# Another order of the seven products of a quad, with folds, scores and combines put at other places, in a channel-attention and squared-ReLU kernel

## The chip, the cores and the metric

The kernel runs on one core of one Trainium2 chip. The metric is device time in microseconds (us) of one execution; of several executions the median counts. One further execution was taken by the hardware profiler, and everything said of engines comes from that one.

## What is computed

For each of four batches a channel attention over 256 channels is followed by a two-layer network with a squared ReLU. Cut to what matters:

```python
qn = q / (norm(q, axis=1) + 1e-6)          # q, k, v: 4 x 6080 x 256
kn = k / (norm(k, axis=1) + 1e-6)
s = kn.transpose(0, 2, 1) @ qn / tau       # 256 x 256 for a batch: the "scores"
a = softmax(s)
x = (v @ a).reshape(24320, 256)
r = maximum(x @ w_in, 0.0)                 # w_in: 256 x 2048
return (r * r) @ w_out                     # w_out: 2048 x 256
```

## The kernel before

**Folding.** The softmax matrix of a batch has only 256 x 256 values, so the kernel never makes x. It multiplies the matrix into w_in (a *fold*) and then works with v and the folded weights. A fold handles one of four groups g of the weights and one of two halves; each half is six matmuls 512 columns wide (line 293).

**Quads and seven products.** The first layer is a 2 x 2 block product computed with seven products in place of eight (a Strassen-like scheme). `combine` (299) makes the seven weight combinations from a folded group, `v_combos` (343) those of v. A *quad* is one (chunk, j): a chunk is two runs of 512 tokens (480 in the last of a batch's six chunks), j counts eight pairs of 128-row blocks of the hidden layer. There are 4 x 6 x 8 = 192 quads. In a quad the functions `m1` to `m7` each issue one product of three matmuls, since every factor is split into a rounded high part and a remainder ("high by high, high by low, low by high"). They accumulate in the PSUM banks B (tile `h`), X (`x`) and Z (`z`), and m7 in a second `h` bank H. Tile pool `h` has two banks; folds, scores, norms and the transposes of the softmax take theirs from the same pool.

**From a product to the second layer.** `block` (381) takes bank X or Z through ReLU and square on ScalarE, then a rounding cast and a subtraction on VectorE, for the hidden blocks "11" and "12". For "21" and "22", `plus_m7` (430) adds m7 to banks B and Z on VectorE into the tile `s`, and `blocks` (392) makes high and low parts: VectorE 398, ScalarE 399, VectorE 400. I call this last sequence the **s chain**. `layer2` (453) multiplies a finished block of the *previous* quad by w_out: three matmuls for each of two halves e. So a quad has 7 x 3 + 8 x 3 = 45 matmuls, all issued in the order of the hand-written list `plan` (608): after each entry `run_side` (597) issues whatever side work is due, by a table of times in units of quads that is filled with `at(...)` (541 to 595).

**Side work.** For a batch that is to come, the scores (`score_burst`, line 182) need the key and query tiles loaded, squares of them summed for the norms (`score_norm`: ScalarE 152, VectorE 153), for batches 2 and 3 a high/low split (`score_split`: ScalarE 158, GpSimd 159), and matmuls (172); then norms, softmax, transposes, folds and combines. For batches 1 to 3 the combine, and the subtraction of `fold_split`, run on GpSimd; for batch 0 on VectorE. The four folds of a batch stand two quads apart, in quads 41, 43, 45 and 47 of the 48 of the batch before, both halves at 0.93 of a quad, followed at once by the combine. The weights w_in and w_out come as 64-bit floats and are decoded (lines 83 to 98) during the first seven quads.

**The head.** Before the first quad the 48 key tiles of batch 0 are scored in 12 groups of four, 1 MB each. Among them stand the decode of the first weight group and, on GpSimd, the combinations and splits of the first chunk of v. Three groups (`EARLY`) of batch 1 are also scored there, between the steps of the softmax; the other nine follow in quads 0 to 8. Loads are issued by SyncE's queue from the list `ring` (474), one after each group, into three buffers `kqt` and two `g2`.

The tile scheduler then reorders instructions within an engine, so their order there can differ from that of the code. On an engine a waiting instruction holds everything behind it.

Of the kernel before, what the change touches and what calls it, by code (L numbers as in the profile page):

```python
# [18 lines left out]
def tile_channel_attention_relu2_ffn(ctx, tc, kq, vT, tau, w_in, w_out, outT):  # L19
# [29 lines left out]
    EARLY = 3  # L49
# [32 lines left out]

    def decode_f64(raw, W):

        top = 122879.9921875
        shape = list(raw.shape[:3])
# [3 lines left out]
        nc.vector.tensor_scalar(out=hw, in0=raw[:, :, :, 1].bitcast(F32), scalar1=top, scalar2=-top,  # L90
                                op0=ALU.min, op1=ALU.max)
        nc.scalar.activation(out=mag, in_=hw, func=AF.Abs, scale=2.0 ** -112)
        nc.scalar.activation(out=low, in_=raw[:, :, :, 0], func=AF.Copy, scale=2.0 ** -29)
# [10 lines left out]
    def raw_tile():  # L104
        return work.tile([P, 2 * NH, GW, 2], U32, name="kqt", tag="kqt", bufs=KB)

    def load_w_in(g):
        raw = raws["in", g] = raw_tile()
        for h in range(NH):
            nc.sync.dma_start(out=raw[:, 2 * h:2 * h + 2].rearrange("p t n two -> p t (n two)"),  # L110
                              in_=wiv[:, h, :, 2 * g * GW:2 * (g + 1) * GW])
# [7 lines left out]
    def load_w_out(g):  # L119
        raw = raws["out", g] = raw_tile()  # L120
        for t in range(2):
            nc.sync.dma_start(out=raw[:, 2 * t:2 * t + 2].rearrange("p j n two -> p j (n two)"), in_=wov[:, g, t])

    def decode_w_out(g):
# [3 lines left out]
        nc.gpsimd.tensor_sub(out=wol[:, g], in0=W, in1=woh[:, g])  # L128
# [143 lines left out]
    def fold_split(b, g):  # L272
        W = win.pop((b, g))
        wi[b, g] = []
        for d in range(NH):
# [65 lines left out]
    ORDER = (A11, S2, A12, S3, A22, S1, S4)  # L341

    def v_combos(ci):

        T = chunks[ci][2]
        eng = nc.vector if ci else nc.gpsimd
# [10 lines left out]
        for i, x in ((A11, lambda: b11), (S2, lambda: t2), (A12, lambda: b21), (S3, lambda: diff(b22, b12)),  # L357
                     (A22, lambda: diff(b21, t2)), (S1, lambda: t1), (S4, lambda: b22)):
            yield ci, i, x

    def v_split(ci, i, x):
# [4 lines left out]
        (nc.vector if ci else nc.gpsimd).tensor_sub(out=t[:, 1, :T], in0=x, in1=t[:, 0, :T])  # L366
# [14 lines left out]
    def block(q, c, ps):  # L381
# [93 lines left out]
    for g in range(NGK):  # L475
        ring.append((score_load, 0, g, "g2" if g % 5 > 2 else "kqt"))
# [172 lines left out]
```

## Time and profile before

| | |
|---|---|
| three runs | 2275.04, 2277.61, 2281.0 us; median 2277.61 |
| the profiled execution | 2273.69 us, span 2271.7 us |
| mean granted TensorE clock | 0.994 |
| busy share of the span | TensorE 97%, VectorE 71%, ScalarE 57%, GpSimd 14% |
| moved by DMA | 329.36 MB, mean 145 GB/s |

The span runs from the first to the last instruction of the program; the 2 us beside it lie around it. "PE" is TensorE's matmul, "DVE" VectorE, "ACT" ScalarE, "POOL" GpSimd, "SP" SyncE, whose queue issues the DMAs. The busy share of PE counts overlapping pipelined matmuls, so time lost between them is partly hidden in the 97%; the prediction goes by counts of matmuls and their pace. In a row of the windows view stand the stretch, its length, then for each engine the busy time and in brackets the number of instructions, at the end the granted clock, the share of DMA engines in use and GB/s. In a row of the groups view stand line, engine, operation, tiles, shapes and count, then after the first bar the busy time of the group in us and the mean of one instruction in ns, and after the second bar the idle time of the engine ahead of them with what ended it.

### The profile page before, as it was taken

The page shows a single profiled execution, that of the slowest core. Times are in us where ns is not written, and L with a number is a line of the kernel's source. Part 1 is how long each engine was busy: PE and PEld are TensorE (multiplying, and loading weights), DVE is VectorE, ACT ScalarE, POOL GpSimd, SP SyncE. Part 2 cuts the span into 40 slices and gives each one's busy share as a digit, 9 for nine tenths or more (in the row PEclk, how much of TensorE's full clock was granted, in tenths as well). Part 3 has the DMA queues.
Part 4 walks back from the last instruction along what each step waited for, and adds up shares of the span by engine and source line. Part 5 has one row for each costly group of instructions (what it writes and reads, how often), then busy time and mean ns, then how long its engine had stood idle before and what let it go on. Part 6 is the DMA issues. An engine that isn't in the chain of part 4 may idle for free.

```text
span 2271.7 us, 25960 instructions
## 1 busy us (share of the span) xinstructions
PE 2199.5 (97%) x9848; PEld 1797.6 (79%) x9848; DVE 1621.8 (71%) x2160; ACT 1294.0 (57%) x2141; POOL 312.9 (14%) x262
## 2 busy tenths in 40 slices
PE   8799999999989999999998999999999999999999
PEld 7578777888868788888886878878887778888887
DVE  6777977567677877877758778787676676666665
ACT  5565755456565665655656556565465555555554
POOL 3000000000442111111053112121114100000000
PEclk9899999999999999999999999999999999999999
DMA  7656633233453433422346344243234432332321
GB/s 287 224 197 259 243 118 126 90 133 127 168 219 118 155 136 110 153 102 103 128 183 221 114 142 156 100 156 113 96 123 180 170 119 98 119 135 83 132 101 65
DMA packets 68860, 329.36 MB, mean 145 GB/s; under 512 B 7424, under 2 KB 11520, under 8 KB 61184
## 3 DMA queue, kind: packets, MB, share of 16 engines
q1 hardware_dynamic: 68736, 327.71, 40.3%
q8 instruction: 77, 1.26, 0.2%
q14 instruction: 47, 0.39, 0.1%
HBM read 271.32 MB, written 56.36 MB: 144 GB/s over the span
## 4 chain that ended last, share of the span: by engine, by line
PE 72%; DVE 8%; DMA 6%; ACT 6%; issue 4%; POOL 3%; SPq 0%; POOLq 0%; ACTq 0%; DVEq 0%
PE o L466 35%; PE h L378 17%; PE z L378 9%; PE x L378 5%; PE h L172 3%; DMA v<-vT 2%; DMA kqt<-kq 2%; DVE g L400 2%; PE h L293 2%; ACT g L399 1%; DMA wsc<-wt 1%; DVE vt L366 1%; POOL wt L315 1%; ACT r L387 1%; ACT r L386 1%
## 5 line engine op out<-in xcount | busy, mean ns | idle before, releaser
L466 PE MATMUL o<-g,woh 128*128 128x512 f32 (+1 forms) x3072 | 1077.1, 391 | 28.9 <-DVE g L400 19.4
L466 PEld LDWEIGHTS o<-g,woh 128*128 128x128 f32 x3072 | 576.8, 188 | 174.2 <-DVE g L400 36.2
L378 PE MATMUL h<-vt,wt 128*128 128x512 f32 (+1 forms) x2304 | 662.1, 391 | 7.7 <-ACT z L417 6.0
L466 PE MATMUL o<-g,wol 128*128 128x512 f32 (+1 forms) x1536 | 596.4, 388 | 1.7 <-POOL wol L128 1.7
L378 PEld LDWEIGHTS h<-vt,wt 128*128 128x128 f32 x2304 | 425.9, 188 | 100.1 <-ACT x L410 9.0
L388 DVE CAST g<-r 128x512 fp32r<-128x512 f32 (+1 forms) x384 | 187.3, 488 | 329.6 <-ACT r L387 328.0
L399 ACT CAST g<-s 128x1024 fp32r<-128x1024 f32 (+1 forms) x192 | 199.6, 1040 | 384.8 <-DVE s L398 384.5
L400 DVE TENSOR_TENSOR g<-s,g 128x1024 fp32r<-128x1024 f32 (+1 forms) x192 | 240.9, 1255 | 145.2 <-ACT g L399 144.9
L378 PE MATMUL z<-vt,wt 128*128 128x512 f32 (+1 forms) x1152 | 329.5, 394 | 12.3 <-DVE s L432 12.1
L466 PEld LDWEIGHTS o<-g,wol 128*128 128x128 f32 x1536 | 288.8, 188 | 58.6 <-POOL wol L128 2.1
L389 DVE TENSOR_TENSOR g<-r,g 128x512 fp32r<-128x512 f32 (+1 forms) x384 | 314.1, 818 | 10.2
L378 PEld LDWEIGHTS z<-vt,wt 128*128 128x128 f32 x1152 | 212.5, 188 | 69.4 <-DVE s L432 29.3
L387 ACT ACTIVATE r<-r 128x512 f32<-128x512 f32 (+1 forms) x384 | 240.5, 626 | 6.6
L398 DVE SCALAR_TENSOR_TENSOR s<-s 128x1024 f32<-128x1024 f32 (+1 forms) x192 | 236.1, 1230 | 5.0
L159 POOL TENSOR_TENSOR hl<-kqt,hl 128x512 fp32r<-128x512 f32 x96 | 139.2, 1463 | 655.8 <-ACT hl L158 655.8
L417 ACT COPY z<-h 128x512 f32<-128x512 f32 (+1 forms) x192 | 109.3, 569 | 192.8 <-PE h L378 191.9
L386 ACT ACTIVATE r<-z 128x512 f32<-128x512 f32 (+1 forms) x192 | 113.1, 589 | 118.7 <-PE z L378 118.7
L432 DVE TENSOR_TENSOR s<-h,m 128x512 f32<-128x512 f32 (+1 forms) x192 | 131.1, 683 | 53.2 <-PE h L378 52.4
L378 PE MATMUL x<-vt,wt 128*128 128x512 f32 (+1 forms) x576 | 164.5, 389 | 0.7 <-ACT x L410 0.7
L153 DVE TENSOR_TENSOR acc<-acc,sq 128x1024 f32<-128x1024 f32 x92 | 116.3, 1264 | 35.0 <-ACT sq L152 33.3
L432 DVE TENSOR_TENSOR s<-z,m 128x512 f32<-128x512 f32 (+1 forms) x192 | 130.7, 681 | 0.0
L386 ACT ACTIVATE r<-x 128x512 f32<-128x512 f32 (+1 forms) x192 | 113.6, 591 | 22.2 <-PE x L378 8.7
(107 smaller groups left out, 1689.6 us busy)
## 6 DMA issues: line engine op xcount, KB each, us to landing
wt<-wsc SPq DMA_DIRECT2D x184, 896.0 KB, 4.6
kqt<-kq SPq DMA_DIRECT2D x55, 1024.0 KB, 5.5
wsc<-wt SPq DMA_DIRECT2D x32, 896.0 KB, 4.5
v<-vT SPq DMA_DIRECT2D x40, 512.0 KB, 4.5
outT<-res SPq DMA_DIRECT2D x80, 256.0 KB, 2.6
kqt<-wins SPq DMA_DIRECT2D x12, 512.0 KB, 5.5
g<-kq SPq DMA_DIRECT2D x4, 1024.0 KB, 11.1
kqt<-w_in SPq DMA_DIRECT2D x8, 512.0 KB, 7.6
```

The source lines that it names most:

```text
L153: nc.vector.tensor_add(out=accs[b], in0=accs[b], in1=sq)
L159: nc.gpsimd.tensor_sub(out=hl[:, 1], in0=x, in1=hl[:, 0])
L378: nc.tensor.matmul(out=out[:, :T], lhsT=w[:, l, i], rhs=v[:, r, :T], start=start and n == 0, stop=n == 2, skip_group_check=True)
L386: nc.scalar.activation(out=r[:, :T], in_=ps[:, :T], func=AF.Relu)
L387: nc.scalar.activation(out=r[:, :T], in_=r[:, :T], func=AF.Square)
L388: nc.vector.tensor_copy(out=hl[:, 0, :T], in_=r[:, :T])
L389: nc.vector.tensor_sub(out=hl[:, 1, :T], in0=r[:, :T], in1=hl[:, 0, :T])
L398: nc.vector.scalar_tensor_tensor(out=s, in0=s, scalar=0.0, op0=ALU.max, in1=s, op1=ALU.mult)
L399: nc.scalar.copy(out=h, in_=s)
L400: nc.vector.tensor_sub(out=l, in0=s, in1=h)
L432: nc.vector.tensor_add(out=state[q]["s"][:, i, :T], in0=ps[:, :T], in1=state[q]["m7"][:, :T])
L466: nc.tensor.matmul(out=o[:, :T], lhsT=l[:, wg, wj, es], rhs=r[:, :T], start=first and k == 0, stop=last and k == 2)
```

## The change

- `plan` has another order. Before: m1, 11, 11, 21, m6, m2, 21, m7, 22, m4, m5, 22, 12, 12, m3. Now: m1, m7, 11, 11, m6, m2, 21, 21, m5, m4, 22, 22, 12, m3, 12 (the blocks are those of the previous quad, one entry for each half e). `blocks` is called from m4, now the later of the two. The v splits are put in the matching order.
- Folds and score bursts are issued at 0.46 of a quad in place of 0.93; the two halves of a fold of batches 1 to 3 stand in two neighbouring quads, and groups are four quads apart in place of two: quads 30 to 44 of a batch in place of 41 to 48. The scores of batches 2 and 3 and the norms of batch 1 end 9 to 11 quads earlier, so they stand closer: one pair of tiles in every quad from 2 to 25, in place of 24 pairs over 35 quads; batch 1's 24 norm steps lie in quads 10 to 25.
- Everything that GpSimd did, but for the score splits of batches 2 and 3, goes to VectorE: combines, `fold_split`'s subtraction, the low part of w_out, the first chunk's v combinations.
- The rounding cast of block "12" goes from VectorE to ScalarE.
- `EARLY` is 8: 32 key tiles of batch 1 are scored in the head. Only two of them stand ahead of the softmax steps, and the first chunk's v combinations are made behind the first combine. `w_in` and `w_out` of group 0 are loaded into buffers of v's pool in place of `kqt`, and `ring` has w_in at place 5 and v at 8.

The diff, cut to what the text speaks of:

```diff
-    EARLY = 3
+    EARLY = 8
...
+        if key[1]:
+            raw = work.tile([P, 2 * NH, GW, 2], U32, name="kqt", tag="kqt", bufs=KB)
...
+        else:
+            parts = raws[key] = [work.tile([P, 2, GW, 2], U32, name="vt", tag="vt", bufs=VB) for _ in range(2)]
...
-        nc.gpsimd.tensor_sub(out=wol[:, g], in0=W, in1=woh[:, g])
+        nc.vector.tensor_sub(out=wol[:, g], in0=W, in1=woh[:, g])
...
-            (nc.gpsimd if b else nc.vector).tensor_sub(out=w[:, 1], in0=x, in1=w[:, 0])
+            nc.vector.tensor_sub(out=w[:, 1], in0=x, in1=w[:, 0])
...
-        eng = nc.gpsimd if b else nc.vector
+        eng = nc.vector
         u = us.pop((b, g))
...
-        nc.vector.tensor_copy(out=hl[:, 0, :T], in_=r[:, :T])
+        eng(out=hl[:, 0, :T], in_=r[:, :T])
...
     def m4(q):
         product(q, A22, state[q]["B"], False)
-        state[q]["s"] = work.tile([P, 2, HMAX], F32, name="s", tag="s", bufs=1)
         plus_m7(q, 0, state[q]["B"])
+        blocks(q)
...
-        block(q, "12", state[q]["Z"])
+        block(q, "12", state[q]["Z"], nc.scalar.copy)
...
-        if g == NGK - 4:
-            for step in v_combos(0):
-                v_split(*step)
...
+    for step in v_combos(0):
+        v_split(*step)
     load_v(1)
-    early_mm(early[8:])
+    early_mm(len(early))
...
-    END = 0.93
+    MID = 0.46
...
-            at(u + END, score_burst, 1, list(range(i * G, i * G + G)))
+            at(u + MID + 0.001, score_burst, 1, list(range(i * G, i * G + G)))
...
-        first, last = (NJ + 3 if b == 1 else 2), QB - 11
+        first, last = (NJ + 2 if b == 1 else 2), 26
...
-            u = end + 2 + 2 * g
-            at(u - 0.9, load_win, b, g)
-            at(u + 0.4, fold_split, b, g)
-            at(u + END, fold, b, g, 0)
-            at(u + END, fold, b, g, 1)
-            at(u + 1.0, combine, b, g)
+            u = end + 4 + 4 * g
+            at(u - 1.5, load_win, b, g)
+            at(u - 0.5, fold_split, b, g)
+            at(u + MID, fold, b, g, 0)
+            at(u + 1 + MID, fold, b, g, 1)
+            at(u + 1.7, combine, b, g)
...
-    plan = (m1, ("11", 0), ("11", 1), ("21", 0), m6, m2, ("21", 1), m7, ("22", 0), m4, m5, ("22", 1), ("12", 0),
-            ("12", 1), m3)
+    plan = (m1, m7, ("11", 0), ("11", 1), m6, m2, ("21", 0), ("21", 1), m5, m4, ("22", 0), ("22", 1), ("12", 0),
+            m3, ("12", 1))
```

What the program has in a row afterwards is shown at three places. The names: `o` are the second layer's accumulators, `g` the high and low parts of a hidden block, `woh` and `wol` those of w_out, `hl` a split, `aTh` and `aTl` the transposed softmax, `u` (in a `kqt` or `vt` buffer) the folded weights, `sq` the combine's sums, `wt` the finished weights of a quad.

First, TensorE at the end of the head, from the last matmuls of the first fold (line 293, in the change 301) to the first products (378, in the change 384). The scores of batch 1 are the rows with `kqt` or `g` alone as their source. Before:

```order
L293 MATMUL h<-hl,aTl 128x512
L172 MATMUL o_374<-kqt 128x256 x8
L378 MATMUL h<-vt,wt 128x512 x3
L378 MATMUL x<-vt,wt 128x512 x3
L378 MATMUL h<-vt,wt 128x512 x9
```

And in the change:

```order
L301 MATMUL h<-hl,aTl 128x512
L179 MATMUL o_353<-kqt 128x256 x10
L179 MATMUL o_353<-g_310 128x256 x8
L179 MATMUL o_353<-g_351 128x256 x8
L384 MATMUL h<-vt,wt 128x512 x9
L384 MATMUL x<-vt,wt 128x512 x3
L384 MATMUL z<-vt,wt 128x512 x3
L384 MATMUL h<-vt,wt 128x512
L179 MATMUL o_353<-kqt 128x256 x8
```

Between the fold and the first product stand 26 score matmuls where 8 stood; another 8, and 16 more a little later, lie among the first quad's matmuls.

Second, TensorE in a quad without side work in the last batch, from m1 on. Before: m1, block 11 in both halves, the first half of block 21, m6, m2:

```order
L378 MATMUL h<-vt,wt 128x512 x3
L466 MATMUL o_16260<-g_16433,woh 128x512
L466 MATMUL o_16260<-g_16433,wol 128x512
L466 MATMUL o_16260<-g_16433,woh 128x512
L466 MATMUL o_16264<-g_16433,woh 128x512
L466 MATMUL o_16264<-g_16433,wol 128x512
L466 MATMUL o_16264<-g_16433,woh 128x512
L466 MATMUL o_16260<-g_16461,woh 128x512
L466 MATMUL o_16260<-g_16461,wol 128x512
L466 MATMUL o_16260<-g_16461,woh 128x512
L378 MATMUL h<-vt,wt 128x512 x3
L378 MATMUL x<-vt,wt 128x512 x3
```

And in the change (m1 and m7 in one row, block 11, m6, m2, the first half of block 21):

```order
L384 MATMUL h<-vt,wt 128x512 x6
L472 MATMUL o_16262<-g_16358,woh 128x512
L472 MATMUL o_16262<-g_16358,wol 128x512
L472 MATMUL o_16262<-g_16358,woh 128x512
L472 MATMUL o_16266<-g_16358,woh 128x512
L472 MATMUL o_16266<-g_16358,wol 128x512
L472 MATMUL o_16266<-g_16358,woh 128x512
L384 MATMUL h<-vt,wt 128x512 x3
L384 MATMUL x<-vt,wt 128x512 x3
L472 MATMUL o_16262<-g_16380,woh 128x512
L472 MATMUL o_16262<-g_16380,wol 128x512
L472 MATMUL o_16262<-g_16380,woh 128x512
```

The first rows of block 21 (source `g_16461` before, `g_16380` now), which need the s chain of the previous quad, stood as the fourth entry of the quad (behind nine matmuls) and stand as the seventh (behind eighteen).

Third, the second combine for batch 1. Before, GpSimd had it, one instruction behind the other:

```order
L307 TENSOR_TENSOR sq<-kqt 128x256
L305 TENSOR_TENSOR sq<-kqt 128x256
L306 TENSOR_TENSOR sq<-sq,kqt 128x256
L308 TENSOR_TENSOR sq<-kqt,sq 128x256
L315 TENSOR_TENSOR wt<-kqt,wt 128x256
L315 TENSOR_TENSOR wt<-kqt,wt 128x128
L315 TENSOR_TENSOR wt<-sq,wt 128x512
```

Now the same work stands on VectorE, among the s chain of a quad (lines 438, 404 and 406 in the change, 432, 398 and 400 before):

```order
L313 TENSOR_TENSOR sq<-kqt 128x256
L438 TENSOR_TENSOR s<-z,m_3778 128x512
L438 TENSOR_TENSOR s<-h,m_3778 128x512
L314 TENSOR_TENSOR sq<-sq,kqt 128x256
L404 SCALAR_TENSOR_TENSOR s<-s 128x1024
L316 TENSOR_TENSOR sq<-kqt,sq 128x256
L406 TENSOR_TENSOR g_3825<-s,g_3825 128x1024
L323 TENSOR_TENSOR wt<-kqt,wt 128x256
L323 TENSOR_TENSOR wt<-kqt,wt 128x128
L323 TENSOR_TENSOR wt<-sq,wt 128x512
```

The combine no longer runs beside VectorE but in its queue, with two of its additions inside the s chain.

More of the change, by code (lines that the diff above doesn't have):

```diff
@@ L89, in decode_f64 @@
         low = work.tile(shape, I32, name="hl", tag="hl", bufs=HB)
-        nc.vector.tensor_scalar(out=hw, in0=raw[:, :, :, 1].bitcast(F32), scalar1=top, scalar2=-top,
-                                op0=ALU.min, op1=ALU.max)
+        n = shape[1] // len(raws)
+        for i, raw in enumerate(raws):
+            part = slice(i * n, (i + 1) * n)
+            nc.vector.tensor_scalar(out=hw[:, part], in0=raw[:, :, :, 1].bitcast(F32), scalar1=top, scalar2=-top,
+                                    op0=ALU.min, op1=ALU.max)
+            nc.scalar.activation(out=low[:, part], in_=raw[:, :, :, 0], func=AF.Copy, scale=2.0 ** -29)
         nc.scalar.activation(out=mag, in_=hw, func=AF.Abs, scale=2.0 ** -112)
-        nc.scalar.activation(out=low, in_=raw[:, :, :, 0], func=AF.Copy, scale=2.0 ** -29)
         mi = mag.bitcast(I32)
@@ L102, in tile_channel_attention_relu2_ffn, with load_f64 @@
     win = {}
-    def raw_tile():
-        return work.tile([P, 2 * NH, GW, 2], U32, name="kqt", tag="kqt", bufs=KB)
+    def load_f64(key, views):
+        if key[1]:
+            raw = work.tile([P, 2 * NH, GW, 2], U32, name="kqt", tag="kqt", bufs=KB)
+            parts = raw[:, :2], raw[:, 2:]
+            raws[key] = [raw]
+        else:
+            parts = raws[key] = [work.tile([P, 2, GW, 2], U32, name="vt", tag="vt", bufs=VB) for _ in range(2)]
+        for part, view in zip(parts, views):
+            nc.sync.dma_start(out=part.rearrange("p j n two -> p j (n two)"), in_=view)
     def load_w_in(g):
[L108 to L111, printed above, removed]
+        load_f64(("in", g), [wiv[:, h, :, 2 * g * GW:2 * (g + 1) * GW] for h in range(NH)])
     def decode_w_in(g):
-        W = work.tile([P, NH, 2, GW], F32, name="sq", tag="sq")
+        tag = "sq" if g else "vt"
+        W = work.tile([P, NH, 2, GW], F32, name=tag, tag=tag, bufs=2 if g else VB)
         decode_f64(raws.pop(("in", g)), W.rearrange("p h t f -> p (h t) f"))
@@ L119, in load_w_out @@
     def load_w_out(g):
-        raw = raws["out", g] = raw_tile()
-        for t in range(2):
-            nc.sync.dma_start(out=raw[:, 2 * t:2 * t + 2].rearrange("p j n two -> p j (n two)"), in_=wov[:, g, t])
+        load_f64(("out", g), [wov[:, g, t] for t in range(2)])
     def decode_w_out(g):
@@ L284, in fold @@
         if ch == 0:
-            us[b, g] = work.tile([P, NH, 2, GW], F32, name="kqt", tag="kqt", bufs=KB)
+            tag, n = ("kqt", KB) if b or g else ("vt", VB)
+            us[b, g] = work.tile([P, NH, 2, GW], F32, name=tag, tag=tag, bufs=n)
         u = us[b, g]
@@ L487, in load_next @@
             step[0](*step[1:])
+            if step[0] is not score_load:
+                load_next()
     for _ in range(5):
@@ L524, in tile_channel_attention_relu2_ffn @@
         exps(0, s0)
-    early_mm(early[4:8])
-    with tc.high_priority():
         attnT(0)
```

58 lines of the change are left out of this document (26 added, 32 removed).

## Prediction

> **What bounds the kernel now.** I read the page first, then the windows view by stretches of the program, then the waits and groups of single stretches.
>
> ```profile
> span 2271.7 us, 25960 instructions
> PE 2199.5 (97%) x9848; PEld 1797.6 (79%) x9848; DVE 1621.8 (71%) x2160; ACT 1294.0 (57%) x2141; POOL 312.9 (14%) x262
> ```
>
> TensorE is the bound, and the change takes no matmul away. So only time between matmuls can be won, and I need to know where that lies. The windows view gives the pace where nothing disturbs, five quads of width 512 and six of width 480 without side work:
>
> ```profile
> 2039.80:2090.80 51.00, 51.00 (x227) 42.23 (x226) 29.96 (x40) 24.89 (x41) 0.00 (x0) 1.00 0.26 91
> 2194.20:2252.70 58.50, 58.50 (x271) 50.59 (x270) 34.40 (x49) 28.50 (x49) 0.00 (x0) 1.00 0.26 88
> ```
>
> A wide quad takes 51.0 / 5 = 10.2 us, a matmul 10.2 / 45 = 0.227, an entry of `plan` 0.68; a narrow quad takes 9.75. A quiet quad has nothing to win. Then the whole program in nine stretches, and the score matmuls (line 172) in three of these:
>
> ```profile
> 0.00:80.35 80.35, 63.37 (x266) 53.45 (x267) 48.40 (x56) 41.81 (x56) 18.53 (x18) 0.92 0.66 255
> 80.35:209.40 129.05, 118.94 (x503) 93.86 (x501) 96.70 (x149) 75.41 (x121) 10.76 (x4) 0.97 0.60 221
> 209.40:550.70 341.30, 338.27 (x1474) 273.49 (x1472) 247.43 (x343) 198.17 (x318) 2.84 (x2) 1.00 0.41 144
> 550.70:674.50 123.80, 114.11 (x500) 93.20 (x500) 89.26 (x118) 75.41 (x139) 50.30 (x49) 0.99 0.54 200
> 674.50:1111.30 436.80, 431.94 (x2013) 354.71 (x2011) 328.50 (x418) 254.75 (x414) 68.25 (x47) 1.00 0.35 124
> 1111.30:1234.90 123.60, 113.00 (x499) 91.79 (x498) 88.20 (x118) 75.43 (x139) 49.93 (x49) 1.00 0.54 200
> 1234.90:1672.80 437.90, 432.23 (x2014) 354.88 (x2013) 328.66 (x418) 254.89 (x414) 68.22 (x47) 1.00 0.35 124
> 1672.80:1791.00 118.20, 111.52 (x498) 91.91 (x498) 84.53 (x114) 68.75 (x130) 44.10 (x46) 1.00 0.52 189
> 1791.00:2271.70 480.70, 476.15 (x2095) 390.29 (x2093) 310.11 (x433) 249.42 (x416) 0.00 (x0) 1.00 0.31 106
> 0.00:80.35 80.35, 57.68 (x240) 48.54 (x240) 0.92 0.66 255
> 80.35:209.40 129.05, 29.85 (x130) 24.09 (x128) 0.97 0.60 221
> 674.50:1111.30 436.80, 38.87 (x288) 38.22 (x288) 1.00 0.35 124
> 9.57 17.55 PE x L172 x80
> ```
>
> From these I take TensorE's floor of each stretch. The last row, of the chain, prices a score record of batches 0 and 1: 17.55 / 80 = 0.219 us.
>
> - Head and quads 0 to 7 (to 209.4): 370 score records at 0.219 (81), eight quads (81.6), four folds of 12 matmuls, the first in the head (48 x 0.227 = 10.9): 173.5. Lost: 36.
> - Quads 8 to 39 (209.4 to 550.7): 32 x 10.2, and four score tiles (4): 330.4. Lost: 11.
> - The three fold stretches (quads 40 to 49 of a batch): eight narrow quads, two wide, four folds: 78 + 20.4 + 10.9 = 109.3. Lost: 14.5, 14.3 and 8.9, together 38.
> - The two score stretches (38 quads each): 387.6 + 38.9 = 426.5. Lost: 10.3 and 11.4, together 22.
> - The rest (46 quads, the last second layer of 24 narrow matmuls at 9.75 / 45 = 0.217): 387.6 + 78 + 5.2 = 470.8. Lost: 10.
>
> Together 117 us, 5% of the time. That is the most that the change could win.
>
> **The change part by part.** *The head.* The waits of TensorE up to 80 us, the last matmul of the fold, the DMA rate at its highest, and VectorE's norm sums:
>
> ```profile
> PE h L201 <- DVE acc L198: 6.9, 1, 6.9
> PE x L172 <- DMA kqt<-kq: 5.3, 3, 3.4
> 63.88 1.84 PE L201 MATMUL h<-ones,acc 128*128 128x1 f32 x8 [6.92 <-DVE acc L198]
> 76.85 0.40 PE L293 MATMUL h<-hl,aTl 128*128 128x512 f32 x1
> 10.00:20.00 10.00, 10.00 (x48) 8.81 (x47) 8.63 (x8) 8.03 (x9) 0.00 (x0) 1.00 1.03 426
> L153 DVE TENSOR_TENSOR acc<-acc,sq 128x1024 f32<-128x1024 f32 x23 | 31.2, 1358 | 23.3 <-ACT sq L152 21.9
> 90.00:100.00 10.00, 6.45 (x17) 4.41 (x18) 9.77 (x14) 5.08 (x7) 0.00 (x0) 0.66 0.82 305
> ```
>
> TensorE needs 16 x 0.219 = 3.5 us for a group of 1 MB, the DMA at 426 GB/s 2.5; so without holes in the issue of loads the last group of batch 0 would be done 11 x 3.5 after 9.57, near 48 us. VectorE's 23 sums take 31.2 us, and stood idle for 23.3 more, because ScalarE's queue held GpSimd's v splits and a load of v. The change takes these out of the head's first part, and the weights' raw tile out of `kqt`. Besides, VectorE has the decode, four passes over 1024 columns, and five subtractions over 512; by the 1358 ns of the row above for 1024 these are at most 4 x 1.36 + 5 x 0.68 = 8.8 us. Sums and these, 40 us, from about 8 on: it ends near 48, and the norm matmul comes at about 50 in place of 63.9. The 13.4 us from there to the fold's end (77.3) are a serial chain and stay: 63.5. Then come the 26 score matmuls (11.4 us, each of two records), during which VectorE makes the combine and the v splits: first products at 75, in place of 80.4 but with two more groups done (7 us). In quad 0 TensorE now stands still half the time (the row 90 to 100: 6.45 busy at a clock of 0.66, VectorE 9.77); the other 24 moved score matmuls (10.5 us) fall in there. What speaks against more: the low part of w_out, 1.2 us, stands in VectorE's queue ahead of the first hidden block, and the last loads wait in SyncE's queue behind the stores of the combine and a load of v that waits for the last split. From quad 4 on the scores no longer cover the decode. Sum: 12.5 + 10.5, less 5 for these: **18 won**; bounds 8 and 25.
>
> *The order of products.* The s chain, with the durations of quiet quads:
>
> ```profile
> L432 DVE TENSOR_TENSOR s<-z,m 128x512 f32<-128x512 f32 x5 | 3.5, 691 | 0.0
> L398 DVE SCALAR_TENSOR_TENSOR s<-s 128x1024 f32<-128x1024 f32 x5 | 6.1, 1227 | 0.2
> L399 ACT CAST g<-s 128x1024 fp32r<-128x1024 f32 x6 | 6.3, 1054 | 20.4 <-DVE s L398 20.4
> L400 DVE TENSOR_TENSOR g<-s,g 128x1024 fp32r<-128x1024 f32 x5 | 6.1, 1225 | 5.6 <-ACT g L399 5.6
> ```
>
> Before, m5 is the 11th entry and ends 7.6 us into the quad; 0.69 + 1.23 + 1.05 + 1.23 later, at 11.8, the low part is there. Block 21 of the next quad needs it in the fourth entry's third matmul, at 10.2 + 2.04 + 0.45 = 12.7. Slack: 0.9 us. Now m4, the 10th entry, is last (7.0), behind m5's sum, which is made at once; the chain ends at 11.2, and block 21 starts with the 7th entry and needs the low part at 14.7. Slack: 3.5 us. In a quiet quad this is worth nothing. Where side work delays VectorE or ScalarE, 2.6 us more are covered. The cast of block 12 costs ScalarE about half of the 1054 ns above, 0.53 us; it has 24.89 / 5 = 5.0 of 10.2 us to do and block 12 is wanted only in the 13th entry of the next quad, so I cost it at nothing. Without that cover it would push the next quad's bank copies by 0.53. The banks speak for the change too: a fold or score issued at 0.46 takes the `h` bank that m7 has left, and the next m7 wants it eight entries or 5.4 us later. At 0.93 both halves of a fold took both banks, and the next quad's m1 had to wait for ScalarE to empty one.
>
> *The folds.* What stops TensorE and ScalarE in the first fold stretch, VectorE's subtraction there, and the start of quad 48:
>
> ```profile
> PE o L466 <- DVE g L400: 4.5, 4, 1.5
> ACT wt L314 <- DMA wsc<-wt: 8.5, 3, 3.3
> L389 DVE TENSOR_TENSOR g<-r,g 128x480 fp32r<-128x480 f32 (+1 forms) x20 | 16.7, 834 | 0.5
> 655.10 1.43 PE L378 MATMUL h<-vt,wt 128*128 128x512 f32 x3 [2.60 <-ACT z L417]
> 655.00:659.00 4.00, 3.90 (x10) 3.12 (x11) 1.94 (x3) 4.00 (x8) 2.01 (x2) 0.57 0.76 302
> ```
>
> The waits are for the s chain, none over 1.5 us, inside the new slack. ScalarE stands up to 3.3 us on the store of the combine's first half, which frees the buffer of the second; in the new order half a quad of other ScalarE work lies between the halves. The hole of 2.6 us at the batch's turn, after which matmuls ran at a clock of 0.57, comes from combine and score splits meeting; now the combine has ended four quads earlier. Against that, VectorE takes over the combine:
>
> ```profile
> L315 DVE TENSOR_TENSOR wt<-sq,wt 128x512 fp32r<-128x512 f32 x4 | 2.6, 687 | 0.1
> L315 DVE TENSOR_TENSOR wt<-kqt,wt 128x256 fp32r<-128x256 f32 (+1 forms) x8 | 2.6, 352 | 0.0
> L307 DVE TENSOR_TENSOR sq<-kqt 128x256 f32<-128x256 f32 x2 | 0.8, 423 | 0.3 <-ACT kqt L296 0.3
> ```
>
> Per group 2 x 0.69 + 4 x 0.35 + 4 x 0.42 = 4.5 us, and two subtractions of the split at 0.69: 5.9 us in four quads, 1.5 a quad on top of 6.0 (29.96 / 5), of which the cast of block 12 (0.43) goes: 7.1 of 10.2, and 1.1 for v. It fits. A piece of it delays the chain by about 1 us, under the slack; on ScalarE three casts in a row can delay a bank copy that TensorE needs early. I leave 14 of the 38 us: **24 won**, bounds 8 and 32.
>
> *The score stretches.* Here POOL still runs the splits, with these rows:
>
> ```profile
> L389 DVE TENSOR_TENSOR g<-r,g 128x512 fp32r<-128x512 f32 x76 | 72.9, 959 | 2.0
> L388 DVE CAST g<-r 128x512 fp32r<-128x512 f32 x76 | 42.4, 558 | 59.5 <-ACT r L387 59.0
> L389 DVE TENSOR_TENSOR g<-r,g 128x512 fp32r<-128x512 f32 x10 | 6.9, 693 | 0.3
> L159 POOL TENSOR_TENSOR hl<-kqt,hl 128x512 fp32r<-128x512 f32 x45 | 65.3, 1465 | 327.5 <-ACT hl L158 327.5
> ```
>
> VectorE's two operations take 0.27 and 0.13 us longer than in quiet quads: 76 x 0.40 = 30 us for 47 POOL operations, 0.64 each. A quad with a score step needs of VectorE 6.0 - 0.4, about 1.9 for the two score sums (one over 1024 columns, one over 512), 1.1 for v (twelve passes at 0.69 in eight quads) and 2 x 0.64: 9.9 of its 10.2 + 38.87 / 24 = 11.8 us. I go by this. The page "SBUF — State Buffer" of the Trainium skill, "Who interferes with whom", speaks of an exclusive lock: a VectorE operation with two SBUF inputs waits for the whole of a GpSimd one. By it the price would be up to 1.47 per POOL operation, VectorE's need 11.5 of 11.8 and this term -5, which makes 2237 of the whole; the trace bears the rule out only in part, with 0.64. The slack helps here, but ScalarE's squares now stand in places ahead of the bank copy that m6 needs, which costs about 1 us each, some eight times a batch. **6 won**, bounds -5 and 15.
>
> *The rest*, quads 8 to 39 and the last 46: the chunk starts get the slack, batch 1's norms lie denser. **4 won**, bounds 0 and 10.
>
> **The rivals.**
>
> *Less of it.* The fold stretches lose to ScalarE's casts and its wait for the store (8.5 us in the row above) as before, and the head's last loads arrive late. Then the lower bounds of head and folds and half of the other two, 8 + 8 + 3 + 2 = 21, up to 30 are won: 2248 to 2257.
>
> *Slower: VectorE becomes the bound of the dense quads.* If each of the two POOL operations of such a quad holds VectorE up for its whole 1465 ns, VectorE needs 11.5 us, and where the chunk's v passes bunch, 12 to 14. Beyond 11.8 each further microsecond is lost in each of 48 quads, since no quad without a score lies between them in which to catch up. At 13 us: 58 lost, the score stretches' 6 not won, head, folds and rest as forecast: 2277.6 - 46 + 58 = 2290. For it speaks that before 14 of 38 quads were free of scores; against it, the 9.9. The page named above is where such a lock is stated.
>
> *Nothing.* VectorE, with all of GpSimd's share, delays quads by as much as the slack gives back, and the loads hold the head: 2272 to 2284.
>
> **How the numbers follow.** 18 + 24 + 6 + 4 = 52. The profiled execution has 2273.7 (span 2271.7), the median is 2277.6, 4 above; I take 52 from the median: 2226. The forecast's own range is 2203 (most terms near their upper bounds) to 2245. Chances: forecast 0.72, less of it 0.19, nothing 0.05 (of which 0.01 beyond 0.3% slower), slower 0.04. The range for 8 in 10 takes in the nearer half of "less of it": 2203 to 2252. About 0.3% (7 us) can be told from no change: faster 0.91, same 0.04, slower 0.05.
>
> **What would show it.** In the profile after: the norm matmul near 50 us, the first products near 75, quad 8's start near 195 (209.4 - 18 + 3.5, since the last group no longer lies in it); fold quads near 10.2 and 11.6 us without waits for the low part of the s chain; VectorE near 9.9 us in a quad with scores. Wrong if VectorE is above 95% busy in the score stretches, if waits for `wt` stores stand in its queue, or if the norm matmul stays near 60.

## The result and the profile after

| | before | after |
|---|---|---|
| median of executions taken side by side | 2276.32 us (4) | 2211.75 us (4) |
| ratio, 95% interval | | 0.9715 [0.9697, 0.9734] |
| the profiled execution | 2273.69, span 2271.7 | 2210.53, span 2208.7 |

64.6 us were won where 52 were forecast; 2211.75 lies inside the range. The head of the page, and TensorE's waits in the whole program (us in total, times, longest):

```profile
span 2208.7 us, 25790 instructions
PE 2174.5 (98%) x9848; PEld 1800.0 (81%) x9848; DVE 1525.9 (69%) x2124; ACT 1398.7 (63%) x2335; POOL 129.8 (6%) x103
```

```profile
PE h L384 <- ACT x L416: 11.8, 19, 2.0
PE z L384 <- DVE s L438: 6.2, 5, 1.3
PE x L179 <- DMA kqt<-kq: 4.6, 2, 3.6
PE o L472 <- ACT g L405: 3.4, 5, 1.6
PE o L472 <- DVE g L406: 1.8, 2, 1.6
```

The waits for the low part of the s chain (`g`, line 400 before, 406 now) are nearly gone. The largest wait that is left is that of the next product for a bank copy on ScalarE (line 416). Where the time went is read from the windows view, cut at the first product of quads 8, 50, 98 and 146. Since the folds now lie in other quads, a stretch here holds a batch's folds and scores together:

```profile
70.05:187.30 117.25, 113.03 (x486) 90.13 (x485) 96.77 (x140) 78.87 (x128) 0.00 (x0) 1.00 0.67 245
187.30:631.10 443.80, 441.81 (x1953) 363.89 (x1952) 323.33 (x466) 294.27 (x498) 4.08 (x3) 1.00 0.45 160
631.10:1184.00 552.90, 541.31 (x2512) 448.73 (x2511) 387.95 (x534) 357.68 (x602) 64.55 (x48) 1.00 0.41 143
1184.00:1731.60 547.60, 539.64 (x2511) 448.86 (x2510) 381.92 (x529) 350.15 (x591) 60.38 (x45) 1.00 0.40 138
1731.60:2208.70 477.10, 473.32 (x2096) 392.18 (x2094) 286.83 (x385) 274.81 (x463) 0.00 (x0) 1.00 0.31 107
```

The same view of every kernel that bears on the cause, in us of a stretch:

| kernel | to quad 8 | 8 to 49 | 50 to 97 | 98 to 145 | the rest | span |
|---|---|---|---|---|---|---|
| before | 209.4 | 465.1 | 560.4 | 556.1 | 480.7 | 2271.7 |
| before, new order alone | 209.7 | 460.4 | 567.7 | 560.3 | 475.0 | 2273.1 |
| before, new places alone | 210.6 | 468.0 | 567.2 | 563.6 | 480.6 | 2290.1 |
| before, combine on VectorE | 208.5 | 454.6 | 551.2 | 549.7 | 480.6 | 2244.6 |
| before, GpSimd idle | 201.6 | 451.0 | 547.8 | 544.8 | 481.3 | 2226.5 |
| after | 187.3 | 443.8 | 552.9 | 547.6 | 477.1 | 2208.7 |
| after, GpSimd idle | 187.6 | 442.0 | 540.8 | 539.2 | 477.1 | 2186.7 |

With the last group of batch 1's scores (3.5 us) counted where it now lies, the change won 25.6 us up to quad 8, 17.8 in quads 8 to 49, 7.5 and 8.5 in the next two stretches and 3.6 in the rest: the 63.0 between the spans. The most is left where GpSimd still works (the column with 64.55 and 60.38 us): by the prediction's floors these two stretches of 48 quads, 426.5 + 109.3 us each, lost 45 us before and still lose 29.

### The profile page after: what moved, and what is told of

Read it like the earlier page. It is cut to its first block, busy times and chain, and to the rows that moved or that the text cites. A ratio compares the mean times of both kernels' runs of the same rounds, so it can differ in the third digit from the quotient of the medians.

```text
span 2208.7 us, 25790 instructions
## 1 busy us (share of the span) xinstructions
PE 2174.5 (98%) x9848; PEld 1800.0 (81%) x9848; DVE 1525.9 (69%) x2124; ACT 1398.7 (63%) x2335; POOL 129.8 (6%) x103
## 4 chain that ended last, share of the span: by engine, by line
PE 73%; issue 14%; DMA 5%; ACT 5%; POOL 3%; DVE 1%; SPq 0%; POOLq 0%; ACTq 0%; DVEq 0%
PE o L472 35%; PE h L384 18%; PE z L384 9%; PE x L384 5%; DMA kqt<-kq 4%; POOL hl L166 3%; PE h L301 2%; PE x L179 2%; PE h L179 2%; PE o L179 1%; ACT sq L159 1%; ACT g L394 1%; ACT hl L165 0%; ACT x L416 0%; ACT r L392 0%
## 5 line engine op out<-in xcount | busy, mean ns | idle before, releaser
L472 PE MATMUL o<-g,woh 128*128 128x512 f32 (+1 forms) x3072 | 1062.4, 388 | 5.6 <-ACT g L405 3.4
L384 PE MATMUL h<-vt,wt 128*128 128x512 f32 (+1 forms) x2304 | 622.5, 392 | 13.3 <-ACT x L416 11.8
L395 DVE TENSOR_TENSOR g<-r,g 128x512 fp32r<-128x512 f32 (+1 forms) x384 | 265.6, 692 | 108.3 <-ACT g L394 103.7
L406 DVE TENSOR_TENSOR g<-s,g 128x1024 fp32r<-128x1024 f32 (+1 forms) x192 | 233.1, 1214 | 142.1 <-ACT g L405 141.4
L394 DVE CAST g<-r 128x512 fp32r<-128x512 f32 (+1 forms) x192 | 81.2, 423 | 265.5 <-ACT r L393 265.3
L404 DVE SCALAR_TENSOR_TENSOR s<-s 128x1024 f32<-128x1024 f32 (+1 forms) x192 | 245.2, 1277 | 4.4
L166 POOL TENSOR_TENSOR hl<-kqt,hl 128x512 fp32r<-128x512 f32 x96 | 129.0, 1362 | 1331.2 <-ACT hl L165 1322.5
L384 PEld LDWEIGHTS x<-vt,wt 128*128 128x128 f32 x576 | 108.2, 188 | 22.5
```

Source lines behind the costliest of these rows:

```text
L166: nc.gpsimd.tensor_sub(out=hl[:, 1], in0=x, in1=hl[:, 0])
L384: nc.tensor.matmul(out=out[:, :T], lhsT=w[:, l, i], rhs=v[:, r, :T], start=start and n == 0, stop=n == 2, skip_group_check=True)
L395: nc.vector.tensor_sub(out=hl[:, 1, :T], in0=r[:, :T], in1=hl[:, 0, :T])
L404: nc.vector.scalar_tensor_tensor(out=s, in0=s, scalar=0.0, op0=ALU.max, in1=s, op1=ALU.mult)
L406: nc.vector.tensor_sub(out=l, in0=s, in1=h)
L472: nc.tensor.matmul(out=o[:, :T], lhsT=l[:, wg, wj, es], rhs=r[:, :T], start=first and k == 0, stop=last and k == 2)
```

## The experiments

Four theories stood against each other. *Slack*: the new order's 2.6 us and the places in the quad let side work pass (what the prediction said). *Places*: the folds lie apart. *Head*: the gain is the early scores. *GpSimd*: what costs is GpSimd's work beside VectorE and ScalarE, and the change helps because it takes most of it away. The first five runs undo one part of the change each (the first one two). All ratios are against the kernel before, measured beside each run; its median lay between 2276 and 2281 us, so the runs are compared by their ratios.

**1. The old order, and everything at 0.93.**

```diff
-    plan = (m1, m7, ("11", 0), ("11", 1), m6, m2, ("21", 0), ("21", 1), m5, m4, ("22", 0), ("22", 1), ("12", 0),
+    plan = (m1, ("11", 0), ("11", 1), ("21", 0), m6, m2, ("21", 1), m7, ("22", 0), m4, m5, ("22", 1), ("12", 0),
...
-    MID = 0.46
+    MID = 0.93
```

> The change with the order of the products, the place of blocks and the order of the v splits as they were, and with side work at 0.93 of a quad (the old order leaves no free bank at 0.46); folds stay four quads apart and on VectorE. Slack theory (the new order gives the s chain 2.6 us more before block 21 wants it): its worth is lost, 20 to 25 us over the change alone, some 2235 us, with waits of TensorE for lines 405 and 406 in quads with folds, scores and chunk turns. Placement theory (folds lost time since they stood together at the batch's end, the order is of no account): no more than the 5 us that the next run loses too, 2212 to 2217.

Measured: 2219.82 us, 0.9733 [0.9719, 0.9748]: 3 us over the placement theory's bound, and far from the 2235 of the slack theory.

**2. The new order, everything at 0.93** (the `MID` line alone).

> The change with side work at 0.93 of a quad in place of 0.46, combine and softmax step moved behind it as far as they must; the new order stays. Slack theory: 2213 to 2220, since the chain has its room wherever the side work stands. Bank theory (at 0.93 a fold or score holds the bank that m1 or m7 of the next quad wants at once): each of some 24 folds, 48 score bursts and 12 other users costs 0.3 to 0.7 us, 2235 to 2260.

Measured: 2215.59 us, 0.9718 [0.9703, 0.9732], within the slack theory's 2213 to 2220 and the change's own ratio. So the place within the quad is worth nothing that can be told, and the order about 4 us (2219.82 against 2215.59; the intervals overlap, and the two profiles differ by 1.3). Of these, 3.6 us in the rest behind quad 145 are plain (480.6 and 477.0 us in the two profiles). TensorE's waits in the second kernel suggest why the place was worth nothing:

```profile
PE h L384 <- DVE s_acc L184: 10.1, 9, 2.0
PE h L384 <- ACT x L416: 3.9, 6, 0.9
```

At 0.93 the score burst's bank is wanted by the next quad's m7, and VectorE's score sum (184) has to empty it: a wait of 10.1 us takes the place of 11.8 - 3.9 for ScalarE's bank copy.

**3. The old places of side work** (scores over 35 quads, folds two quads apart with both halves together).

```diff
-        first, last = (NJ + 2 if b == 1 else 2), 26
+        first, last = (NJ + 3 if b == 1 else 2), QB - 11
...
-            u = end + 4 + 4 * g
+            u = end + 2 + 2 * g
```

> The change with the table of side work for batches 1 to 3 as it was: folds in quads 41 to 47, two quads apart, both halves at 0.93, scores of 24 pairs over 35 quads at 0.93; new order, all on VectorE. Slack theory: the fold quads still have the 2.6 us, 2218 to 2225. Placement theory: the three fold stretches lose again what they lost before less GpSimd's share, 25 us and more: 2237 to 2245.

Measured: 2221.82 us, 0.9739 [0.9723, 0.9755]: some 5 us lost, not clear of the change's interval, and within the slack theory's 2218 to 2225. The 25 us of the placement theory did not appear.

**4. Combine and the fold split's subtraction back on GpSimd** for batches 1 to 3.

```diff
-        eng = nc.vector
+        eng = nc.gpsimd if b else nc.vector
```

> The change with combine and fold_split's subtraction of batches 1 to 3 on GpSimd again, 12 groups. If the new slack is what counts, VectorE's longer operations beside GpSimd (about 0.6 us per GpSimd operation) hide: 2210 to 2217. If taking GpSimd out was what freed the fold stretches, 12 groups lose some 1.5 us each: 2225 to 2235.

Measured: 2225.25 us, 0.9759 [0.9744, 0.9773]: 10 us lost, the most of these and the only loss clear of the intervals; it is at the edge of what was expected if GpSimd counts (2225 to 2235). The wait for the bank copy has doubled:

```profile
PE h L384 <- ACT x L416: 22.6, 28, 2.1
```

**5. Three early groups in place of eight.**

```diff
-    EARLY = 8
+    EARLY = 3
```

> The change with 3 groups of batch 1 scored in the head in place of 8; the other nine in quads 0 to 8 as before, everything else as in the change. If the moved scores fill holes in the head and quad 0 (theory of the prediction, 10 of its 18 us): 2219 to 2224. If the head was won by taking GpSimd's work and w_in's buffer out of the loads' way alone: 2211 to 2214.

Measured: 2215.99 us, 0.9726 [0.9709, 0.9742]: 2.5 us, not clear of the intervals, between the two expectations. The first products come at 62.9 us, but quad 0 then waits for the decode, and quad 8 starts at 190.8 with one group of scores fewer behind it. With that group's 3.5 us this is 7.0 later than the change's 187.3. The two score stretches, in which nothing was altered, took 548.6 and 546.4 us in place of 552.9 and 547.6, which hides most of the 7.0. So a stretch can move by some 4 us from one program to the next without an edit in it, and losses of that size in a single stretch say little.

Undone one at a time the parts are worth 4 + 0 + 5 + 10 + 2.5, about 22 of 65 us. Part of what is missing was never undone (the head's loads, buffers and v steps); behind quad 7 it is 19 of 37 us. Parts may also cover for one another, so from the next run on parts were made alone.

**6. Before, with the first chunk's v behind the first combine and on VectorE.**

```diff
-        if g == NGK - 4:
-            for step in v_combos(0):
-                v_split(*step)
...
         combine(0, 0)
+    for step in v_combos(0):
+        v_split(*step)
```

> The kernel before with one edit: the first chunk's v combinations and splits stand behind the first combine, on VectorE, in place of the head's middle on GpSimd. If they held ScalarE and VectorE and so the norm sums: the norm matmul comes 5 to 8 us earlier than 63.9 and the time is 2268 to 2272. If the loads hold the head (w_in's raw tile in kqt stays): the norm matmul comes no more than 3 us earlier, and VectorE's v work falls into the first quad: 2275 to 2280.

Measured: 2270.03 us, 0.9969 [0.9956, 0.9982]: 7 us, as the first expectation had it, with the norm matmul at 58.1 in place of 63.9, the first products at 74.9 in place of 80.35 and quad 8 at 204.2 in place of 209.4.

**7. The change, with the score splits on VectorE as well**, so that GpSimd has nothing to do behind the start.

```diff
         nc.scalar.copy(out=hl[:, 0], in_=x)
-        nc.gpsimd.tensor_sub(out=hl[:, 1], in0=x, in1=hl[:, 0])
+        nc.vector.tensor_sub(out=hl[:, 1], in0=x, in1=hl[:, 0])
```

> The change with the score splits of batches 2 and 3 on VectorE too, so that GpSimd does nothing there. VectorE gets 2 x 0.69 us per quad with a score and is rid of 2 x 0.64 us of GpSimd's blocking: by this sum nothing moves, 2208 to 2215. If GpSimd holds VectorE for its whole operation (2 x 1.4 us): 48 quads gain, 2195 to 2205. If VectorE is near its bound there: 2220 and more.

Measured: 2187.79 us, 0.9605 [0.9591, 0.9619]: 24 us faster than the change, the fastest kernel here, by more than any theory had. Quads 50 to 71 in the change (windows view, then VectorE's groups):

```profile
631.10:902.60 271.50, 260.68 (x1255) 216.47 (x1254) 188.30 (x226) 175.82 (x284) 58.57 (x44) 1.00 0.37 128
```

```profile
L404 DVE SCALAR_TENSOR_TENSOR s<-s 128x1024 f32<-128x1024 f32 x22 | 33.1, 1507 | 0.6
L395 DVE TENSOR_TENSOR g<-r,g 128x512 fp32r<-128x512 f32 x44 | 31.8, 722 | 10.9 <-ACT g L394 10.3
L372 DVE TENSOR_TENSOR vt<-tt,vt 128x512 fp32r<-128x512 f32 x11 | 8.5, 772 | 2.9 <-ACT vt L371 2.9
L372 DVE TENSOR_TENSOR vt<-v,vt 128x512 fp32r<-128x512 f32 x8 | 7.7, 960 | 1.0 <-ACT vt L371 0.7
```

And with the splits on VectorE:

```profile
629.60:889.10 259.50, 259.18 (x1255) 216.47 (x1254) 196.69 (x270) 172.00 (x284) 0.00 (x0) 1.00 0.39 134
```

```profile
L395 DVE TENSOR_TENSOR g<-r,g 128x512 fp32r<-128x512 f32 x44 | 30.3, 689 | 7.8 <-ACT g L394 7.4
L404 DVE SCALAR_TENSOR_TENSOR s<-s 128x1024 f32<-128x1024 f32 x22 | 26.8, 1218 | 0.0
L372 DVE TENSOR_TENSOR vt<-tt,vt 128x512 fp32r<-128x512 f32 x11 | 7.6, 688 | 2.8 <-ACT vt L371 2.8
L372 DVE TENSOR_TENSOR vt<-v,vt 128x512 fp32r<-128x512 f32 x8 | 5.5, 686 | 0.9 <-ACT vt L371 0.9
```

VectorE's operations were 22 x 0.289 + 44 x 0.033 + 11 x 0.084 + 8 x 0.274 = 11 us longer beside GpSimd's 44, 0.25 each, and the stretch 12 us. Without GpSimd VectorE is busy for 196.69 us, 8.4 more, TensorE waits for nothing, and VectorE still has a quarter of the time free. One reservation: with other durations in view the scheduler also put ScalarE's and TensorE's instructions of these quads in another order. ScalarE's cast 405 waited 20 times for 404 in the change (56.3 us in all) and once in run 7 (3.7), because there a ReLU stands ahead of it; and the squares waited for their loads seven times (3.3 us) and then not at all. So the 24 us are the lengthening, the other order and any effect on the loads together.

**8. Score bursts at 0.2 of a quad.** The change's remaining wait, around the start of quad 55 at 691.1 us and in it (timeline view, in brackets what ended the idle time before):

```profile
688.68 1.55 DVE L404 SCALAR_TENSOR_TENSOR s<-s 128x1024 f32<-128x1024 f32 x1
690.26 1.05 ACT L405 CAST g<-s 128x1024 fp32r<-128x1024 f32 x1 [3.02 <-DVE s L404]
...
694.07 1.06 ACT L159 ACTIVATE sq<-kqt 128x1024 f32<-128x1024 f32 x1 [1.59 <-DMA kqt<-kq]
...
695.54 0.61 ACT L394 CAST g<-r 128x512 fp32r<-128x512 f32 x1
696.06 0.57 ACT L416 COPY x<-h 128x512 f32<-128x512 f32 x1
...
696.69 0.97 PE L384 MATMUL h<-vt,wt 128*128 128x512 f32 x3 [1.98 <-ACT x L416]
...
700.95 3.00 POOL L166 TENSOR_TENSOR hl<-kqt,hl 128x512 fp32r<-128x512 f32 x2 [11.80 <-ACT hl L165]
701.40 1.40 DVE L395 TENSOR_TENSOR g<-r,g 128x512 fp32r<-128x512 f32 x1
702.72 1.78 DVE L372 TENSOR_TENSOR vt<-v,vt 128x512 fp32r<-128x512 f32 x1
705.15 0.96 PE L384 MATMUL z<-vt,wt 128*128 128x512 f32 x3 [1.26 <-DVE s L438]
```

Here the square (159), which waits for its load, stands ahead of the bank copy (416) that m6 needs, and so does the cast of block 12 (394), which the change moved to ScalarE; and where two of GpSimd's operations run, two of VectorE's take 1.40 and 1.78 us in place of 0.69 and a sum is late. I thought that 1.4 us of score matmuls ahead of m6 would cover the copy.

```diff
-                at(u + MID, score_burst, b, [k, k + 1])
+                at(u + 0.2, score_burst, b, [k, k + 1])
```

> The change with the score bursts of batches 2 and 3 at 0.2 of a quad in place of 0.46, between block 11 and m6. Theory: what is left in the score stretches is m6 waiting for ScalarE's copy of bank B, made late when a square stands ahead of it; 1.4 us of score matmuls ahead of m6 cover that: about 12 us less, 2198 to 2203, and no waits for line 416 in these stretches. Rival (VectorE's sums and GpSimd's blocking are what is late): the wait only moves to the score matmuls or to m3, 2208 to 2216.

Measured: 2219.56 us, 0.9745 [0.9725, 0.9764], 7 us slower (the intervals just overlap); both expectations failed. The wait for the copy stayed, and the burst, now behind m7, waits for ScalarE to empty m7's bank:

```profile
PE h L384 <- ACT x L416: 10.9, 19, 1.7
PE h L179 <- ACT m L434: 9.1, 14, 0.8
```

The loads came later too: in quads 50 to 71 ScalarE's squares waited for them for 29.7 us, 3.3 in the change. And the lengthened operation was another one. Line 404 was back at its quiet time, but the bank copy was waited for as before:

```profile
L404 DVE SCALAR_TENSOR_TENSOR s<-s 128x1024 f32<-128x1024 f32 x21 | 25.7, 1224 | 0.7
L394 DVE CAST g<-r 128x512 fp32r<-128x512 f32 x22 | 13.7, 623 | 27.6 <-ACT r L393 27.6
```

The last four runs put single parts of the change into the kernel before.

**9. Before, with the new order alone** (`plan`, `blocks` called from m4, v splits in that order).

> The kernel before with the new order of products alone (the blocks called from m4, the v splits in the matching order); side work, engines and head as they were. Slack theory, as the prediction had it: the s chain's 2.6 us of slack alone end the waits of the fold stretches for it, and the chunk starts gain: 15 to 22 us, 2254 to 2261. Overlap theory, from the run with the old order in the changed kernel (worth 4 there): each part covers what the others cover, so that taken alone one of them can bring more than it costs to take away; then 8 to 15 us, 2261 to 2268. GpSimd theory (what delays VectorE and ScalarE is GpSimd beside them, and the order only covers a little of it): about 4 us, 2270 to 2274.

Measured: 2275.03 us, 0.9982 [0.9972, 0.9991]: 4 us, what the GpSimd theory had (the profiled execution does not show them, its span is 1.4 us longer than before). TensorE's waits in the whole program:

```profile
PE h L378 <- ACT x L410: 16.3, 13, 2.2
PE h L378 <- DVE s_acc L177: 14.5, 12, 2.2
```

The 19.4 us of waits for the s chain's low part that the kernel before had are gone, as the slack theory said, and 31 us of waits for `h` banks stand in their place. I take the reason to be that m7 now comes second in the quad, so that both banks are needed early. The table shows 4.7 and 5.7 us won in quads 8 to 49 and in the rest, 7.3 and 4.2 lost in the two stretches with score bursts.

**10. Before, with the new places alone**, all still at 0.93.

```diff
-        first, last = (NJ + 3 if b == 1 else 2), QB - 11
+        first, last = (NJ + 2 if b == 1 else 2), 26
...
-            u = end + 2 + 2 * g
+            u = end + 4 + 4 * g
```

> The kernel before with the new places of side work alone (folds four quads apart and their halves in two quads, scores in quads 2 to 25, everything still at 0.93 of a quad, combine on GpSimd). If folds one behind the other are what costs in the fold stretches: 15 to 20 us won there, 2256 to 2262. GpSimd theory: its combine and splits delay VectorE as often as before wherever they stand, and the score quads lie denser with the small slack of the old order: 0 to 8 us won, 2268 to 2276.

Measured: 2292.66 us, 1.0059 [1.0044, 1.0074]: slower by 13 us, outside both expectations. TensorE's waits, and VectorE's subtraction in the dense quads 50 to 71, which took 693 ns in quiet quads:

```profile
PE o L466 <- DVE g L400: 22.8, 47, 1.2
PE z L378 <- DVE s L432: 18.6, 23, 1.2
```

```profile
L389 DVE TENSOR_TENSOR g<-r,g 128x512 fp32r<-128x512 f32 x44 | 50.3, 1142 | 1.1
```

VectorE's operations beside GpSimd are lengthened, but that is not where the time went. The quads with scores (50 to 73 and 98 to 121) took 292.7 and 293.2 us, no more than in the change (294.9 and 292.0): 9.0 and 9.5 over the floor of 283.7 that the prediction's terms give (24 x 10.2 + 38.9). So the prediction's slower rival, 58 us lost in these quads, is not seen. The quads with folds lost the time: 24 to 49, 74 to 97 and 122 to 145 took 297.1, 274.5 and 270.4 us, 65 over their floors of 272.5, 252.1 and 252.1, and the change loses 15 there. In quads 74 to 97 the waits are for VectorE's sums (5.0 us), the s chain's low part (3.7) and ScalarE's cast (2.2). The change with the combine on GpSimd (run 4) loses 29 in these quads, with the order, the cast and the place in the quad of the change. So folds that lie apart are no gain by themselves while GpSimd combines, and the new order with what goes with it covers a good part of that loss.

**11. Before, with combine, fold split and w_out's low part on VectorE.**

```diff
-        eng = nc.gpsimd if b else nc.vector
+        eng = nc.vector
         u = us.pop((b, g))
```

> The kernel before with the combine, the subtraction of the fold's split and the low part of w_out on VectorE; score splits and the first chunk's v stay on GpSimd. GpSimd theory: some 130 operations fewer beside VectorE, by the 0.25 us each of the run without score splits 33 us, of which the batch turns and fold stretches can give at most their 38: 15 to 30 won, 2247 to 2262. Rival, VectorE's room: with folds two quads apart and a slack of 0.9 us the combine in VectorE's own queue delays the s chain as much as GpSimd did: 0 to 6 won, 2270 to 2276.

Measured: 2246.37 us, 0.9855 [0.984, 0.987]: 33 us won by this part alone (27 by the spans of the two profiles), with the folds two quads apart and the old slack; a little more than the GpSimd theory's best. What happened at the batch's turn (quad 48) in the kernel before:

```profile
646.88 1.75 POOL L307 TENSOR_TENSOR sq<-kqt 128x256 f32<-128x256 f32 x1 [12.15 <-ACT kqt L296]
...
653.48 0.62 ACT L314 CAST wt<-sq 128x512 fp32r<-128x512 f32 x1 [4.54 <-POOL sq L308]
...
654.45 0.59 ACT L417 COPY z<-h 128x512 f32<-128x512 f32 x1
```

GpSimd's four small additions and a split between them last from 646.9 to 653.4; ScalarE's cast (314) waits 4.54 us for the last of them, and behind it stands the bank copy (417) for which TensorE then waits 2.60 us. On VectorE those additions take 0.42 to 0.70 us each. VectorE's subtraction 400 in the narrow quads took, before and now,

```profile
L400 DVE TENSOR_TENSOR g<-s,g 128x960 fp32r<-128x960 f32 x8 | 11.7, 1469 | 7.1 <-ACT g L399 7.1
L400 DVE TENSOR_TENSOR g<-s,g 128x960 fp32r<-128x960 f32 x8 | 9.3, 1158 | 4.7 <-ACT g L399 4.7
```

and TensorE's waits for its result in quads 40 to 49 fell from 4.5 to 0.5 us. These quads took 123.8 us before and now

```profile
549.60:663.10 113.50, 110.78 (x498) 92.07 (x498) 95.55 (x162) 73.93 (x136) 4.45 (x3) 1.00 0.61 217
```

**12. Before, with all of GpSimd's work on VectorE** (run 11, the score splits, and run 6's v).

```diff
-        nc.gpsimd.tensor_sub(out=hl[:, 1], in0=x, in1=hl[:, 0])
+        nc.vector.tensor_sub(out=hl[:, 1], in0=x, in1=hl[:, 0])
```

> The kernel before with all of GpSimd's work on VectorE, score splits too, and the first chunk's v combinations and splits behind the first combine; order, places and number of early groups as they were. GpSimd theory: 6 for the head's v, 24 for the splits and 15 to 25 for the combines, 45 to 55 in all: 2221 to 2231, so most of what the change brings without its order and its places. Rival: without the order's slack VectorE's longer queue delays the s chain in score and fold quads, and little but the head's 6 and half the splits' 24 is left: 2250 to 2260.

Measured: 2227.77 us, 0.9775 [0.9757, 0.9793]: 51 us won, as the GpSimd theory had it, without new order, places or early groups.

## Why the prediction was right, and where its reasons were not

**Head: 18 forecast, 25.6 measured.** The mechanism held, its size was too small:

```profile
48.01 0.95 PE L208 MATMUL h<-ones,acc 128*128 128x1 f32 x8
```

```profile
70.05 0.81 PE L384 MATMUL h<-vt,wt 128*128 128x512 f32 x2
```

The norm matmul comes at 48.0 (forecast 50) and waits for nothing, the first products at 70.05 (75), quad 8 at 187.3 (195). Of the 7.6 us beyond the forecast 5 lie ahead of the first products: 2 before the norm matmul, and 2.2 in "a serial chain" from there to the fold's end, which was to stay at 13.4 us and took 11.2 (the fold ends at 59.2). The others lie in quads 0 to 7, where the term "less 5 for these" was too much. A part that the sum did not name is the granted clock: 0.92 and 0.97 before in the two stretches up to quad 8, 1.00 in the change. TensorE's busy time times what the clock lacked, over stretches of ten us, comes to some 6 us before (2.2 of it from 90 to 100 us) and to none now; that is an estimate, and no run parts it from the rest. Run 6 gives v's part as some 5 to 7 us; run 5 shows first products at 62.9 with the same three early groups that run 12 has at 74.1, so 11 us come from what these two differ in, the raw weights' buffers, the loads' order and two score tiles ahead of the softmax. These three were not run apart. That the early scores themselves fill quad 0 was right: run 5 prices them at 7.0 us up to quad 8, of the 10.5 that the sum had.

**Folds: 24 forecast; the size about right, the cause wrong.** By their floors the quads 24 to 49, 74 to 97 and 122 to 145 lose 5.7, 5.9 and 3.6 us in the change, 15 where the forecast left 14 of 38. That this came out was in part luck, since the forecast gave the gain to the new order's slack. The step that failed is "the waits are for the s chain, none over 1.5 us, inside the new slack": the waits were there, but what made the chain late was GpSimd, and taking its combine away all but ended them (run 11) with the old order and the old slack. The new order alone (run 9) left quads 40 to 49 at 125.0 us against 123.8; the new places alone lost time; taking the combine from GpSimd alone won 10.3 us there, and 10.5, 9.2 and 6.4 in the three stretches of the table that hold folds. The 2.6 us hole at the turn, which I put down to "combine and score splits meeting", was ScalarE waiting for GpSimd's additions, with a split between them; that reading was right as far as it went. The forecast of fold quads without waits held, and so did the price of the combine on VectorE; TensorE's only wait in quads 24 to 49 of the change is

```profile
PE z L384 <- DVE s L438: 1.2, 1, 1.2
```

**Score stretches: 6 forecast.** Here the change brought some 2 us: quads 50 to 73 and 98 to 121 took 294.9 and 292.0 us, 11.2 and 8.3 over the floor of 283.7, where 22 were lost before. What I got wrong is how GpSimd's price is paid. I set 0.64 us per operation against VectorE's free time (9.9 of 11.8 us) and found room. VectorE had more room than that (188.30 / 22 = 8.6 us busy in a quad), and TensorE waited all the same. Run 7 took no more than 0.25 us of lengthening per operation from VectorE and still won 24 us. That the longer operations delay a chain (404, ScalarE's cast 405 behind it, the squares and bank copies behind that) is read from one quad and not shown: in run 8 line 404 had its quiet 1224 ns, and the waits for the copy stayed. "SBUF — State Buffer" in the Trainium skill, "Who interferes with whom", states the exclusive lock by which I worked out -5 in place of 6 for this term; that it lasts for the whole of an instruction the page says of VectorE's two-port modes, and of operations with two SBUF inputs that they contend. Single rows come near a whole one (1.78 us in place of 0.69 beside a pair of GpSimd's that took 3.00), the mean does not reach it (0.25 here; (1142 - 693) x 44 / 42 = 0.47 of this line alone in run 10). As a warning against the splits that the change left on GpSimd, the page was worth more than my weighing of it. The bank copy behind the squares was waited for 19 times, 11.8 us in all, a little less each than the 1 us forecast.

**The rest: 4 forecast, 7.7 measured, by the mechanism that was forecast.** Quads 24 to 39, which hold folds now, are left out of this. Of the 7.7 us 3.6 lie in the last 46 quads. A quiet quad takes 10.20 us in both orders, and the chunk starts get the slack: the three quads around one (151 to 153) took 10.5, 11.0 and 10.55 us before, 10.41, 10.38 and 10.20 in the change. The last 46 quads took 480.6 to 481.3 us in every kernel with the old order, 477.0 or 477.1 in every one with the new order and the cast on ScalarE. The cast of block 12, costed at nothing on ScalarE, costs some 2 us there: run 9 has the new order with the cast on VectorE, 475.0 us and 10.20 in those three quads. The other 4.1 us lie in quads 8 to 23, ahead of the folds (173.2 us less the moved 3.5 before, 165.6 now); no run shows what they come from.

**What stays open.** From run 12 to run 7, both with GpSimd idle, 40 us of span lie: with the moved group counted as above 17.5 up to quad 8, 18.1 in the quads to 145 and 4.2 in the rest. In the middle ones order, places and cast together bring what order and places did not bring in runs 9 and 10. Which of them needs which was not tried without GpSimd's work. Nor is run 7's gain divided between lengthened operations and the order in which the scheduler put ScalarE's queue, and the combine's move, too, ended both at once: GpSimd's slow additions in ScalarE's path and its lengthening of VectorE.

## What to carry to other kernels

Work on a "free" engine is not free when its results are waited for in another engine's queue: look at who waits for it and what stands behind the waiting instruction, before asking whether the receiving engine has room. A part that loses little when it is undone may still bring much, since other parts cover for it; add it alone to the kernel before as well. And a new order that ends one wait should be read for the resource that it now asks for early, here the two `h` banks.

## What the hardware showed unexpectedly

Beside a GpSimd subtraction on SBUF tiles VectorE's operations were lengthened, and which one was hit differed from program to program: before it was line 389 (959 ns in place of 693) and, less, the cast 388 (558 in place of 427), in the change the 1024-column line 404 (1507 in place of 1218), with the bursts at 0.2 the cast 394 (623 in place of 424). Moving 96 subtractions of 1.35 us from GpSimd to a VectorE that was 69% busy, with the scheduler's new order that came with it, made the program 24 us faster.
